# Late products of a fused attention and feed-forward kernel: four PSUM tiles of one bank in place of two tiles of two banks

## The chip, the core and the metric

The kernel runs on one core of a Trainium2 chip. A core has a matrix engine (TensorE, called PE in the profile, with its weight loads as PEld), three engines that work on vectors (VectorE or DVE, ScalarE or ACT, GpSimd or POOL), and SyncE (SP), which here issues the DMAs. PE writes its results into PSUM, a small memory of eight banks; a bank holds 512 float32 values in each of 128 partitions. VectorE and ScalarE read them from there. The metric is the time of one execution on the device in microseconds (us), as the median over executions.

## The reference

Two blocks follow each other. The first is a gated linear recurrence over 768 steps for 4 batches and 8 heads with a head dimension of 48; the second is a feed-forward network with a product of two branches.

```python
f = 1.0 / (1.0 + np.exp(-f_logit))
for t in range(S):
    state = f[:, :, t, :, None] * state + np.einsum('bhd,bhe->bhde', k[:, :, t], v[:, :, t])
    y[:, :, t] = np.einsum('bhd,bhde->bhe', q[:, :, t], state)
...
x = np.ascontiguousarray(y.transpose(0, 2, 1, 3)).reshape(B * S, H * D)   # 3072 x 384
a = x @ w1                    # 3072 x 1024
b = x @ w2
h = a * b @ w3
return (h @ w_out).astype(np.float32)
```

The inputs of attention are float32. The four weights arrive as float64 and are turned into float32 on the core (`fetch`, L1378) before they are used. The result is float32.

## The kernel before, in words

**Stages.** The 3072 tokens are 24 units of 128 tokens (`u`), six for each batch, and six blocks of 512 tokens (`n`). Attention works unit by unit: products of keys and queries inside a unit, a mask, products with the values, and a state that is carried to the next unit. When four units are done, their outputs form a block, and the feed-forward network works on the block. The weights w3 and w_out are multiplied with each other once (`fold`), so that only one output product per block remains.

The feed-forward products of a block are computed in one of three ways. Block 0 uses plain products (`part`). Blocks 1 and 2 use a scheme of seven products in place of eight (`seven`, L972). Blocks 3 to 5 use a scheme that combines sums of slices of x and of w into 18 products, each accumulated in a chain, and adds up their results (`many`, L1120; products at L1148, copies out of PSUM by ScalarE at L1169, additions by VectorE at L1192, the final products of a and b at L1204 and L1211). The output of each block comes from `down` (L1232). It opens three banks, named X, Y and Z, with `start`; the products m1 to m7 go through `three` (L894), so that all of them carry line 897 in the profile. ScalarE copies (`k1`, L1269; `c11`, L1282) and VectorE adds (L1275, L1288, L1299, L1305, L1313) empty those banks.

Beside that work, ScalarE reads through all weights again in the late stretch (`ranges`, L1520, lines 1536 and 1540) to judge whether their size allows this way of computing; if not, a general path is run afterwards.

**The order.** The order of all instructions is written by a planner (`Plan`). A task names its engine, an estimated cost, a priority, what it depends on, and what it takes and frees of counted resources. The planner lists the tasks in time by these estimates, and the loop at L1626 emits them in that order; the program keeps it on every engine. The waits between engines are added afterwards from what each instruction reads and writes of the kernel's tiles.

**The banks.** The resource "f" counts places in PSUM. It has four places (`NF`) during attention, each a tile of one bank in the pool `ps_f`, with the names f0 to f3. The other four banks belong to attention: the pool `ps` has two tiles, `pa` and `py`, each of two banks (`[P, 2, NQ]` with `NQ` = 512). The tile pa holds the products of keys and queries (L579) and the updates of the state (L686), py the outputs of a unit (L653, L672). When the last unit is planned (`u == NU - 1`, L1601 to L1605), four more places are added to "f". They come free when that unit's last tasks on pa and py end: `y` (ScalarE's copy at L845), `mid` (VectorE, L759), `m` (ScalarE, L703) and `v`.

A product that gets one of the first four places asks `ps_f` for a new tile at each opening. A product that gets a later place gets a half of a tile that was made once, at the first such product, and is used by all that follow: places 4 and 5 are the two halves of `pa`, places 6 and 7 the two halves of `py`. The function that hands out the places is `bank` (L378). It runs while instructions are emitted, when the order is already fixed:

```python
if plan.got >= NF:
    nm = ("pa", "py")[(plan.got - NF) // 2]
    if nm not in found:
        found[nm] = ps.tile([P, 2, NQ], F32, name=nm)
    return found[nm][:, plan.got % 2]
return ps_f.tile([P, TB], F32, name=f"f{plan.got}")
```

In the profile the late products into these four banks therefore stand under the names pa and py, with the lines 993 (`seven`), 1148 (`many`) and 897 (`down`); the names do not tell the half. In these rows a product 256 columns wide is written twice side by side and read as 512 wide, and a product of `down` is 192 wide.

Of the kernel before, what the change touches and what calls it, by code (L numbers as in the profile page):

```python
# [36 lines left out]
F32 = mybir.dt.float32  # L37
# [8 lines left out]
P = 128  # L46
# [9 lines left out]
TB = 512  # L56
# [3 lines left out]
NQ = HP * C  # L60
# [3 lines left out]
NF = 4  # L64
# [185 lines left out]
@with_exitstack  # L250
def kernel(
    ctx: ExitStack,
    tc: tile.TileContext,
    q: bass.AP,
    k: bass.AP,
    f_logit: bass.AP,
    v: bass.AP,
    w1: bass.AP,
    w2: bass.AP,
    w3: bass.AP,  # L260
    w_out: bass.AP,
    leaf_mask: bass.AP,
    out: bass.AP,
):
    nc = tc.nc
    const = ctx.enter_context(tc.tile_pool(name="const", bufs=1))
    ident = const.tile([P, P], F32, name="ident")
    w12 = const.tile([P, 2, 2, KM, KH * P], F32, name="w12")
    wc = const.tile([P, KF, DM], F32, name="wc")
    left = const.tile([1, 1], I32, name="left")  # L270
    with tc.manual_schedule():
        outside = ranged(tc, q, k, f_logit, v, w1, w2, w3, w_out, out, ident, w12, wc, left)
        with tc.If(outside > 0, preferred_fallthrough_block=True, label="general"):
            if w1.dtype != F32:
                convert(tc, w1, w2, w3, w_out, w12, wc)
            general(tc, q, k, f_logit, v, leaf_mask, out, ident, w12, wc)
# [17 lines left out]
def ranged(ctx, tc, q, k, f_logit, v, w1, w2, w3, w_out, out, ident, w12, wc, left):  # L294

    nc = tc.nc
    PSUM = bass.MemoryType.PSUM
# [7 lines left out]
    outs = ctx.enter_context(tc.tile_pool(name="outs", bufs=4))  # L305
    one = ctx.enter_context(tc.tile_pool(name="one", bufs=1))
    dram = ctx.enter_context(tc.tile_pool(name="dram", bufs=3, space=bass.MemoryType.DRAM))
    ps = ctx.enter_context(tc.tile_pool(name="ps", bufs=1, space=PSUM))
    ps_f = ctx.enter_context(tc.tile_pool(name="ps_f", bufs=1, space=PSUM))

    floors = keep.tile([P, NQ], F32, name="floor")
    floor = floors[0:R]
# [45 lines left out]
    found = {}  # L358
# [7 lines left out]
    plan = Plan()  # L366
# [11 lines left out]
    def bank():  # L378

        if plan.got >= NF:  # L380
            nm = ("pa", "py")[(plan.got - NF) // 2]
            if nm not in found:
                found[nm] = ps.tile([P, 2, NQ], F32, name=nm)
            return found[nm][:, plan.got % 2]
        return ps_f.tile([P, TB], F32, name=f"f{plan.got}")

    def temporary(i):
# [196 lines left out]
    def turn(u):  # L584

        s = st[u]
        if u < NPE:
            s["py"] = ps.tile([P, 2, NQ], F32, name="py")
            s["pk"] = s["py"][:, :, 2 * C : 2 * C + 2 * R]
        else:  # L590
            s["pk"] = bank()[:, 0 : HP * R].rearrange("p (b r) -> p b r", b=2)
        for hp in range(HP):
            nc.tensor.transpose(  # L593
                out=s["pk"][:, hp // 2, hp % 2 * R : hp % 2 * R + R], in_=s["K"][:, hp * C : hp * C + C],
                identity=ident[0:R, 0:R],
            )

    def first_values(u):

        s = st[u]  # L600
        opens = u % NCH == 0
        s["yb"] = bank().rearrange("p (h c) -> p h c", c=C)[0:R]
        for hp in range(HP):
            for par in range(2):
                h = 2 * hp + par
                w = 64 if par == 0 else D
                nc.tensor.matmul(
                    s["yb"][64 * par : 64 * par + w, hp], lhsT=s["v"][:, h * D : h * D + w],
                    rhs=s["A"][:, par, hp], start=hp == 0, stop=opens, skip_group_check=True,
                )  # L610
        if not opens:
            for hp in range(HP):
                nc.tensor.matmul(
                    s["yb"][:, hp], lhsT=sb[(u - 1) % 2][:, hp], rhs=s["Q"][:, hp * C : hp * C + C],
                    start=False, stop=True, skip_group_check=True,
                )
# [151 lines left out]
    def rest(u):  # L768
# [102 lines left out]
        def moved():  # L871
            s["px"] = bank()[:, 0 : KM * C].rearrange("p (k c) -> p k c", c=C)
            for i, (kc, hp) in enumerate(met):
                nc.tensor.matmul(
                    s["px"][:, kc], lhsT=perm[:, i], rhs=s["ys"][:, hp], start=i % 2 == 0, stop=i % 2 == 1,
                )
# [710 lines left out]
    for u in range(NU):  # L1587
# [13 lines left out]
        if u == NU - 1:  # L1601
            late = plan.add("none", 0.0, lambda: None)
# [408 lines left out]
```

## Time and profile before

| what | value |
| --- | --- |
| median of 4 runs | 463.29 us (463.14 to 463.96) |
| the profiled execution | 463.43 us |
| its span, first to last instruction | 461.7 us, mean granted TensorE clock 0.998 |
| PE busy over the span | 453.4 us |
| VectorE, ScalarE, GpSimd busy | 361.6, 208.8, 66.0 us |
| last unit's copy out of py (L845) | starts at 255.62 us |
| first late product into pa, into py | 264.21 us, 267.66 us |
| last product ends | about 457.3 us |

All times inside the span are counted from its first instruction. A row of the timeline gives a start, a length, the engine, the line, the operation, what is written and what is read (`out<-in`), the shape and how many instructions were merged into the row. In square brackets stands how long the engine was idle before the row and what released it. The list of waits gives, for an engine and a line, who was waited for, the total in us, how often, and the longest wait. The table by stretch gives the window, its length, and for PE, PEld, DVE, ACT and POOL the busy time and the number of instructions, then the granted clock, the share of DMA time and the GB/s moved. Matmuls are pipelined, so one that takes 0.38 us can follow the one before after less than that.

### The profile page before, as it was taken

What the parts mean: (1) busy time and instruction counts of PE and PEld (TensorE: products, weight loads), DVE (VectorE), ACT (ScalarE), POOL (GpSimd) and SP (SyncE); (2) the same over time, 40 slices, a digit from 0 to 9 for tenths busy, and PEclk for the clock granted to TensorE, in tenths of its full rate; (3) what the DMA queues carried; (4) which work ended last, traced back from release to release, by engine and by line L of the source; (5) the groups of instructions that cost most, each with busy time, mean ns of one, the idle gap of its engine ahead of it and who ended that gap; (6) DMA issues with size and microseconds to landing.
All of it is one profiled execution on the core that took longest, in us unless ns stands there. A gap on an engine that the chain in (4) does not pass through costs nothing.

```text
span 461.7 us, 11749 instructions
## 1 busy us (share of the span) xinstructions
PE 453.4 (98%) x4800; PEld 395.9 (86%) x4800; DVE 361.6 (78%) x633; ACT 208.8 (45%) x468; POOL 66.0 (14%) x90
## 2 busy tenths in 40 slices
PE   8999999999999999999999999999999999999996
PEld 6788885666899888889998888998898988889995
DVE  8996999999898999988983599895658566868551
ACT  3565334432234453443323256575665666673000
POOL 9340000121223431223222000000000000000000
PEclk9999999999999999999999999999999999999999
DMA  6997898833246764356323326643265523200111
GB/s 182 280 317 229 310 331 288 267 105 104 70 111 185 209 179 135 102 140 185 99 65 99 128 87 212 214 150 117 97 193 173 179 84 92 92 2 0 36 69 39
DMA packets 43309, 68.75 MB, mean 149 GB/s; under 512 B 5217, under 2 KB 28386, under 8 KB 42226
## 3 DMA queue, kind: packets, MB, share of 16 engines
q1 hardware_dynamic: 43250, 67.95, 47.8%
q8 instruction: 39, 0.64, 0.6%
q14 instruction: 20, 0.16, 0.1%
HBM read 58.88 MB, written 9.04 MB: 147 GB/s over the span
## 4 chain that ended last, share of the span: by engine, by line
PE 95%; DVE 2%; SPq 1%; DMA 1%; issue 0%; POOL 0%; POOLq 0%; DVEq 0%
PE f L897 25%; PE f L993 15%; PE f L1148 11%; PE f L1464 9%; PE py L1148 6%; PE pa L1148 5%; PE py L897 4%; PE pa L897 4%; PE py L653 3%; PE pa L579 2%; PE pa L686 2%; PE f L593 2%; PE py L672 2%; PE py L993 1%; PE f L399 1%; SPq L492 1%
## 5 line engine op out<-in xcount | busy, mean ns | idle before, releaser
L709 POOL TENSOR_SCALAR_AFFINE_SELECT A<-A 64x512 f32<-64x512 f32 (+1 forms) x46 | 43.8, 952 | 109.3 <-ACT A L703 107.1
L1464 PE MATMUL f<-place 128*128 128x384 f32 x128 | 42.4, 487 | 0.0
L897 PE MATMUL f<-xt,w 128*128 128x256 f32 x192 | 42.1, 380 | 0.0
L897 PEld LDWEIGHTS f<-xt,w 128*128 128x128 f32 x192 | 36.3, 190 | 5.0
L1464 PEld LDWEIGHTS f<-place 128*128 128x128 f32 x128 | 23.9, 190 | 15.5
L993 PE MATMUL f<-xt,w 128*128 128x256 f32 x140 | 36.2, 380 | 0.0
L897 PE MATMUL f<-place 128*128 128x192 f32 x192 | 34.8, 327 | 0.0
L897 PEld LDWEIGHTS f<-place 128*128 128x128 f32 x192 | 31.5, 190 | 0.3 <-issue 0.2
L548 DVE TENSOR_TENSOR_SCAN bwd<-gate,back 112x512 f32<-112x512 f32 x24 | 30.4, 1267 | 0.7
L526 DVE TENSOR_TENSOR_SCAN fwd<-gate,floor 112x512 f32<-112x512 f32 x24 | 30.0, 1251 | 1.1 <-ACT gate L518 0.2
L993 PEld LDWEIGHTS f<-xt,w 128*128 128x128 f32 x140 | 26.3, 190 | 3.5
L845 ACT ACTIVATE ys<-py 112x512 f32<-112x512 f32 x22 | 13.1, 596 | 32.6 <-PE py L672 29.7
L1400 ACT ACTIVATE place<-place 128x512 f32<-128x512 uint32 (+2 forms) x24 | 21.4, 890 | 9.8 <-DMA place<-in_w_dram 7.9
L897 PE MATMUL f<-wc,ab 128*128 128x192 f32 x128 | 23.6, 328 | 0.0
L809 POOL TENSOR_TENSOR G<-lasts,gate 112x4 f32<-112x4 f32 x20 | 11.6, 582 | 75.6 <-ACT lasts L531 30.2
L993 PE MATMUL f<-place 128*128 128x256 f32 x84 | 22.4, 385 | 0.0
L518 ACT ACTIVATE gate<-f 112x512 f32<-112x512 f32 x22 | 13.9, 632 | 17.4 <-DMA f<-in_f_logit_dram 8.1
L897 PEld LDWEIGHTS f<-wc,ab 128*128 128x128 f32 x128 | 21.3, 190 | 0.4
L653 PEld LDWEIGHTS py<-A,vt 64*64 64x64 f32 (+1 forms) x672 | 13.3, 127 | 7.3 <-issue 6.5
L653 PE MATMUL py<-A,vt 64*64 64x64 f32 (+1 forms) x672 | 18.1, 223 | 0.2
L1540 ACT ACTIVATE A<-A,back 128x512 f32<-128x512 f32 x23 | 17.9, 780 | 0.2
L1262 DVE TENSOR_TENSOR place<-ab 128x512 f32<-128x512 f32 x24 | 16.6, 690 | 1.0 <-PE f L897 0.9
(355 smaller groups left out, 1046.1 us busy)
## 6 DMA issues: line engine op xcount, KB each, us to landing
place<-in_w_dram SPq DMA_DIRECT2D x21, 512.0 KB, 6.4
A<-in_w_dram SPq DMA_DIRECT2D x19, 512.0 KB, 3.8
place<-in_w_dram SPq DMA_DIRECT2D x8, 1024.0 KB, 6.6
q<-in_q_dram SPq DMA_DIRECT2D x46, 96.0 KB, 2.8
vt<-in_v_dram SPq DMA_DIRECT2D x23, 192.0 KB, 3.4
out_dram<-o SPq DMA_DIRECT2D x23, 192.0 KB, 2.2
k<-in_k_dram SPq DMA_DIRECT2D x44, 96.0 KB, 2.4
yt<-ys SPq DMA_DIRECT2D x44, 96.0 KB, 2.7
```

The costliest lines, as they stand in the source:

```text
L518: nc.scalar.activation(gate[u % 2][:, 0:NQ], fu, AF.Sigmoid)
L526: nc.vector.tensor_tensor_scan(s["P"], gate[u % 2][:, 0:NQ], floor, 0.0, ALU.mult, ALU.max)
L548: nc.vector.tensor_tensor_scan(s["R"][:, ::-1], gate[u % 2][:, NQ:0:-1], back[:, ::-1], 0.0, ALU.mult, ALU.max)
L653: done = nc.tensor.matmul(y_block(u, hp, par, half)[p0 : p0 + w], lhsT=s["v"][half * W : half * W + W, h * D : h * D + w], rhs=s["A"][half ...
L709: nc.gpsimd.affine_select(out=a, in_=a, pattern=pattern, compare_op=ALU.is_ge, fill=0.0, base=0, channel_multiplier=-1,)
L897: nc.tensor.matmul(out_, lhsT=lhs[i], rhs=rhs[i], start=start and i == 0, stop=i == len(lhs) - 1, skip_group_check=True,)
L993: nc.tensor.matmul(q[nm][:, which * TH : which * TH + TH], lhsT=lhs[i](which), rhs=rhs[i], start=start and which == 0 and i == 0, stop=i = ...
L1148: nc.tensor.matmul(banks[g, c][:, which * TH : which * TH + TH], lhsT=lhs, rhs=x_node(a), start=first and which == 0, stop=True, skip_grou ...
L1262: nc.vector.tensor_tensor(abs_[j], x, y, op)
L1400: nc.scalar.activation(part_.bitcast(F32), part_, AF.Copy, bias=2.0, scale=2.0**-51)
L1464: nc.tensor.matmul(w3s["p", jc], lhsT=w3s[jc][:, kc * P : kc * P + P], rhs=wos[:, kc], start=(kc == 0), stop=(kc == KF - 1),)
L1540: return lambda: nc.scalar.activation(a, a, AF.Sign, bias=small, accum_out=counts[:, i : i + 1])
```

## The change

The pools are opened in another order, `ps_f` first, and `ps` is opened in an exit stack of its own, so that it can be closed early. At the first late product, `bank` closes `ps`, and a pool `ps_late` is opened on the banks that come free. From then on each product that gets one of the places 4 to 7 asks `ps_late` for a new tile of one bank, named l4 to l7, as the products in the first four places do with `ps_f`. The planner, its resources and the order of the instructions are not touched.

```diff
-    ps = ctx.enter_context(tc.tile_pool(name="ps", bufs=1, space=PSUM))
     ps_f = ctx.enter_context(tc.tile_pool(name="ps_f", bufs=1, space=PSUM))
+    pairing = ExitStack()
+    ps = pairing.enter_context(tc.tile_pool(name="ps", bufs=1, space=PSUM))
...
     def bank():
 
         if plan.got >= NF:
-            nm = ("pa", "py")[(plan.got - NF) // 2]
-            if nm not in found:
-                found[nm] = ps.tile([P, 2, NQ], F32, name=nm)
-            return found[nm][:, plan.got % 2]
+            if "late" not in found:
+                pairing.close()
+                found["late"] = ctx.enter_context(tc.tile_pool(name="ps_late", bufs=1, space=PSUM))
+            return found["late"].tile([P, TB], F32, name=f"l{plan.got}")
         return ps_f.tile([P, TB], F32, name=f"f{plan.got}")
```

## The prediction

> **What bounds the kernel now.** I read the page first: engine shares, slices, chain.
>
> ```profile
> PE 453.4 (98%) x4800; PEld 395.9 (86%) x4800; DVE 361.6 (78%) x633; ACT 208.8 (45%) x468; POOL 66.0 (14%) x90
> ...
> PE   8999999999999999999999999999999999999996
> ...
> PE 95%; DVE 2%; SPq 1%; DMA 1%; issue 0%; POOL 0%; POOLq 0%; DVEq 0%
> ```
>
> TensorE is busy 98% of the span and 95% of the chain that ended last is its work. Only an interval in which PE stands still can be won. So the second view is the list of waits of PE in the late stretch, 262 us to the end, which is all that the change touches:
>
> ```profile
> PE py L897 <- DVE ys L1192: 0.6, 1, 0.6
> ```
>
> It has one entry: one product into py, waiting once, for a VectorE addition. The busy table by stretch says the same:
>
> ```profile
> 256.30:457.26 200.96, 200.39 (x1038) 184.00 (x1036) 138.06 (x282) 103.64 (x241) 0.00 (x0) 1.00 0.34 110
> ```
>
> The first number after the window is its length, the second PE's busy time: 0.57 us idle in 201 us, at a full clock (1.00). The third view is the timeline around that place:
>
> ```profile
> 352.89 1.89 PE L1148 MATMUL f<-place,f 128*128 128x256 f32 x8
> ...
> 353.16 0.69 DVE L1192 TENSOR_TENSOR a<-pa,a 128x512 f32<-128x512 f32 x1 [0.98 <-PE pa L1148]
> ...
> 354.61 0.69 DVE L1192 TENSOR_TENSOR ys<-ys,py 128x512 f32<-128x512 f32 x1
> ...
> 355.35 1.57 PE L897 MATMUL py<-wc,ab 128*128 128x192 f32 x8 [0.57 <-DVE ys L1192]
> ```
>
> The x8 group before the hole spans 1.89 us and one matmul lasts 0.379 (the row of L1148), so its starts are (1.89 - 0.379) / 7 = 0.216 us apart. Its last start is 352.89 + 7 x 0.216 = 354.40, and the next product could have begun at 354.62. It began at 355.35, when the addition that reads py ended (354.61 + 0.69 = 355.30).
>
> Is that wait a need of the data? The product at 355.35 is the first of an output block (m1 in `down`). It opens a bank, so it only needs that bank's last reader. The rows of py just before tell which one that was:
>
> ```profile
> 336.88 1.03 PE L1148 MATMUL py<-xt,q 128*128 128x256 f32 x4
> ...
> 346.83 1.46 PE L897 MATMUL py<-place,ab 128*128 128x192 f32 x8
> 348.63 0.35 DVE L1305 TENSOR_TENSOR o<-py,place 128x192 f32<-128x192 f32 x1
> ```
>
> Two products live in py at once: the 512-wide one, last written at 336.88 and read only at 354.61, and a 192-wide output product that opened, grew and was read (348.63 to 348.98) in between. One bank cannot hold both, so they are py's two halves. The half with the output product was free from 348.98 on; its operand ab was complete before too, since the sums over the same ab (L1262) had run by 348.71 (348.02 + 0.69). The wait at 355.35 is for the other half. The tie between the halves shows a second time, 40 us earlier:
>
> ```profile
> 311.84 1.03 PE L1148 MATMUL py<-place,floor 128*128 128x256 f32 x4
> ...
> 312.91 0.36 DVE L1313 TENSOR_TENSOR o<-py,place 128x192 f32<-128x192 f32 x1 [1.81 <-PE py L1148]
> 313.30 0.59 ACT L1169 COPY ys<-py 128x512 f32<-128x512 f32 x1 [3.15 <-DVE o L1313]
> ```
>
> VectorE, with the output product complete, stands until a product in the other half ends; then ScalarE, which only reads, waits for VectorE, which only reads. A tile of two banks is guarded as one thing where the halves' uses overlap.
>
> **The change, part by part.**
>
> *The tie goes.* Each late product now has a tile of its bank alone. At 355.35 PE no longer waits for the addition: 355.35 - 354.62 = 0.73 us. The group behind the hole also took 1.57 us where the same group takes 1.46 elsewhere (346.83), because its weights were loaded only as the wait ended: 0.11 us more. Sum 0.84.
>
> *Near misses.* Where ScalarE is held behind VectorE as above, its copy lands just before PE's next accumulation into that bank: the copy from pa at 386.27 ends 386.86 and the product starts at 387.00, and of the eight matmuls pa<-xt,fwd the longest takes 391 ns against a median of 379. Some four such places at 10 to 15 ns: 0.05 us. I take it in.
>
> *What is late next.* VectorE has no idle row from 353.16 to its addition L1288 at 362.15, which PE's product at 362.82 waits for; VectorE stood 0.60 us before 362.15, so it is free at 361.55. With PE 0.84 earlier, the product would be due at 361.98 and L1288 would end at 361.55 + 0.36 = 361.91: still in time, with 0.07 in hand. And VectorE itself gets the 0.98 us back that it stood at 353.16 for a product in pa while it read the half that was not being written. I take a loss of 0, with 0.3 as the upper end should VectorE run late all the same. Further on the waits for ScalarE's copies are 0.9 us short of mattering in the regular pattern (a copy of 0.59 us starts as PE begins the following product, and PE comes back two products of 0.86 later).
>
> *Freed waits of VectorE and ScalarE.* In this stretch they are busy 138.06 and 103.64 of 200.96 us. PE waits for them nowhere else, so what they gain is worth nothing on the path. Covered by PE's work.
>
> *New tile per product.* 33 products open in pa and py after 262 us. Each of them becomes a fresh tile that must wait for the release of the one before in its bank, by all that touched it, PE itself included. Lower end: nothing, as for the products in f, which already work so; their groups run at the same 0.216 and (1.46 - 0.326) / 7 = 0.162 us as those in pa and py, with 0.0 idle. Upper end: every opening loses its overlapped weight load as at 355.35, 33 x 0.11 = 3.6 us. Below nothing it cannot go, since a wait added gives no time back. I take nothing; f is the same operation on the same engine.
>
> *The hand-over.* The pool of pa and py closes and the new one opens on its banks, so the first late product may wait for all of attention's readers: the last is ScalarE's copy L845, 255.62 to 256.31. The first product into pa starts at 264.21. Cover 7.9 us, cost nothing; without the planner's own hold on these four slots it would be at most that.
>
> *Order and queues.* `bank()` is called when the order is already fixed, so no instruction changes its place on PE, DVE, ACT, POOL or SP; no DMA is added or moved. The order of the two PSUM pools changes, so the tiles sit in other banks; all eight are in use before and after. Bounds 0 and 0.
>
> Sum: 0.84 + 0.05 = 0.89 us. The profiled execution took 463.43 us: 461.7 of span and 1.73 around it, which stays. 463.43 - 0.89 = 462.54. The median of the runs shown is 463.29, 0.14 below it: 462.4.
>
> A rule against reading it so. PE's starts 0.216 and 0.162 us apart in f, pa and py alike say that it works at its own rate and only the hole is to be had, 0.89 us. The Trainium skill ("Perfetto Trace Analysis", section "Identifying the Most-Contended Engine") calls matmul busy time a poor measure of headroom and asks for the share of weight loads instead. By it the late stretch has 200.96 - 184.00 = 16.96 us of room, and a change that loosens waits could win up to that.
>
> **The rivals.**
>
> *No change.* The halves are not what ties them, or the released tile carries the same wait: 463.3. For it: the profile names tiles, not banks. Against it: rows 311.84 to 313.30, where one reader waits for another.
>
> *Slower: openings pay.* Each of the 33 openings loses the prefetched weight load, 3.6 us: 463.29 - 0.89 + 3.6 = 466.0. It decides against the change from 0.89 / 0.11 = 8 openings on. For it: after the hole the load was late by 0.11. Against it: the openings in f.
>
> *Larger gain.* Freed engines let PE close more than I see. PE has 0.57 us idle by the table and 0.89 by its starts; more would need stops that neither shows. The tail behind 457.26 (last addition 457.30, last store issued 457.69) is a chain behind PE and only shifts. If as much again as the 0.89 went: 461.5.
>
> **How the numbers follow.** 0.2% of 463.29 is 0.93 us, about what a measurement of this kernel can tell from no change, and the forecast of 0.89 lies on that line. Chances: forecast 0.74 (462.1 to 462.8, the 0.3 of VectorE and the spread of the runs), larger gain 0.06, no change 0.10, openings pay 0.10. Of the forecast's 0.74 I put 0.42 beyond 0.93 us, since a freed VectorE and ScalarE can only remove further small misses, and 0.32 short of it. Faster 0.42 + 0.06 = 0.48, same 0.32 + 0.10 = 0.42, slower 0.10. The range takes in no change and leaves out the larger gain and most of the slower case: 462.0 to 463.6.
>
> **What would show it.** In the profile after: the list of PE's waits after 262 us without the row for py L897, the output group near 354.6 at 1.46 us instead of 1.57, and all later rows 0.8 to 0.9 us earlier; no row in which ACT L1169 is released by a DVE addition that only reads another product; idle before the late products 0.0. Wrong would be: a new row of PE waiting at an opening, gaps at 264, or the group at 362 starting late behind L1288.

## The result and the profile after

The changed kernel takes 462.46 us (median of 33 runs), the kernel before 463.35 us (median of 53). The ratio is 0.998, with a 95% interval of 0.9973 to 0.9987: a gain of 0.9 us, clear of zero, and just short of the 0.2% (0.93 us) that the prediction took as the line between faster and no change. Forecast was 462.4 us.

The profiled execution after the change took 462.61 us with a span of 460.8 us. Its page, in the lines that answer to those of before (engines, PE's slices, the chain by engine):

```profile
PE 452.6 (98%) x4800; PEld 396.3 (86%) x4800; DVE 362.4 (79%) x633; ACT 208.6 (45%) x468; POOL 67.8 (15%) x90
...
PE   7999999999999999999999999999999999999996
...
PE 95%; POOL 2%; DVE 1%; issue 0%; POOLq 0%; DVEq 0%
```

Nothing of the picture changes at this scale: the same 4800 matmuls, PE busy 98%. The difference stands in PE's waits. Before, the late stretch had one. This is the whole list of PE's waits after the change, over the whole span (engine, line, who was waited for; then us in total, times, longest):

```profile
PE f L400 <- DVE floor L423: 1.7, 1, 1.7
PE py L594 <- DVE K L557: 0.6, 1, 0.6
PE pa L687 <- issue: 0.6, 1, 0.6
PE f L594 <- DVE K L557: 0.4, 1, 0.4
```

All four belong to attention and its start; the lines are one higher than before, since the diff adds a line above them. The late stretch has none left. Its row in the table by stretch (window, length, PE busy, PEld, DVE, ACT, POOL, clock, DMA share, GB/s):

```profile
256.30:456.40 200.10, 200.10 (x1038) 184.66 (x1037) 138.24 (x282) 104.07 (x242) 0.00 (x0) 1.00 0.34 111
```

PE was idle 0.57 us of 200.96 before, and is idle 0.00 of 200.10 now. The two windows do not hold quite the same work, because attention took 0.12 us longer in this execution: the first late product starts at 264.33, where it was 264.21. Counted from the start of the first late product to the end of the last product (457.27 before, 456.51 now), PE's same 1000 matmuls take 193.06 us before and 192.18 now, 0.88 us less. This stretch is free of attention's small differences, and the experiments below are compared by it too.

The timeline around the hole:

```profile
352.14 1.03 PE L1149 MATMUL l<-place,bwd 128*128 128x256 f32 x4
352.22 0.68 DVE L1193 TENSOR_TENSOR a<-l,a 128x512 f32<-128x512 f32 x1
...
353.01 1.89 PE L1149 MATMUL f<-place,f 128*128 128x256 f32 x8
...
353.66 0.69 DVE L1193 TENSOR_TENSOR ys<-ys,l 128x512 f32<-128x512 f32 x1
...
354.73 1.46 PE L898 MATMUL l<-wc,ab 128*128 128x192 f32 x8
```

Two things moved. The output group starts 354.73 - 353.01 = 1.72 us after the group before it, where it was 355.35 - 352.89 = 2.46: 0.74 us. And it takes 1.46 us in place of 1.57: 0.11 us. That is 0.85 of the 0.88 us. The other 0.03 are three matmuls, at 387.00, 400.83 and 404.29 before, that took 391, 387 and 392 ns; no matmul of their groups takes more than 380 now. The second movement around the hole is easy to pass over: VectorE's first addition, a<-l,a, now starts at 352.22, beside the product with bwd that PE is just writing to the other bank. Before, it started at 353.16, after 0.98 us of standing, 0.27 us after the matching PE group ahead of the hole. It now starts 0.79 us ahead of that group (353.01). So the addition that PE used to wait for ends at 354.35, before PE arrives.

The other place that the prediction showed has lost its two ties:

```profile
311.96 1.03 PE L1149 MATMUL l<-place,floor 128*128 128x256 f32 x4
312.16 0.36 DVE L1314 TENSOR_TENSOR o<-l,place 128x192 f32<-128x192 f32 x1 [0.94 <-PE l L898]
...
313.03 0.58 ACT L1170 COPY ys<-l 128x512 f32<-128x512 f32 x1 [2.73 <-PE l L1149]
```

VectorE is released by the output product that it reads (L898), and starts at 312.16, while PE writes the other bank; before it waited until that write had ended. ScalarE is released by the product that it reads, and no longer by VectorE.

### The profile page after: what moved, and what is told of

It is laid out like the page before. It is cut to its first block, busy times and chain, and to the rows that moved or that the text cites. A ratio compares the mean times of both kernels' runs of the same rounds, so it can differ in the third digit from the quotient of the medians.

```text
span 460.8 us, 11785 instructions
## 1 busy us (share of the span) xinstructions
PE 452.6 (98%) x4800; PEld 396.3 (86%) x4800; DVE 362.4 (79%) x633; ACT 208.6 (45%) x468; POOL 67.8 (15%) x90
## 4 chain that ended last, share of the span: by engine, by line
PE 95%; POOL 2%; DVE 1%; issue 0%; POOLq 0%; DVEq 0%
PE f L898 25%; PE f L994 15%; PE f L1149 11%; PE l L1149 11%; PE f L1465 9%; PE l L898 8%; PE py L654 3%; PE pa L580 2%; PE pa L687 2%; PE f L594 2%; PE l L994 2%; PE py L673 2%; POOL ab L438 1%; PE f L400 1%; DVE K L557 0%
## 5 line engine op out<-in xcount | busy, mean ns | idle before, releaser
L898 PE MATMUL f<-xt,w 128*128 128x256 f32 x192 | 42.1, 380 | 0.0
L898 PEld LDWEIGHTS f<-xt,w 128*128 128x128 f32 x192 | 36.4, 190 | 4.9
L898 PE MATMUL f<-place 128*128 128x192 f32 x192 | 34.8, 327 | 0.0
L898 PEld LDWEIGHTS f<-place 128*128 128x128 f32 x192 | 31.5, 190 | 0.3 <-issue 0.2
L810 POOL TENSOR_TENSOR G<-lasts,gate 112x4 f32<-112x4 f32 x20 | 12.6, 630 | 76.3 <-ACT lasts L532 28.9
L898 PE MATMUL f<-wc,ab 128*128 128x192 f32 x128 | 23.6, 328 | 0.0
L898 PEld LDWEIGHTS f<-wc,ab 128*128 128x128 f32 x128 | 21.3, 190 | 0.4
L654 PE MATMUL py<-A,vt 64*64 64x64 f32 (+1 forms) x672 | 18.1, 223 | 0.2
```

The costliest lines, as they stand in the source:

```text
L654: done = nc.tensor.matmul(y_block(u, hp, par, half)[p0 : p0 + w], lhsT=s["v"][half * W : half * W + W, h * D : h * D + w], rhs=s["A"][half ...
L898: nc.tensor.matmul(out_, lhsT=lhs[i], rhs=rhs[i], start=start and i == 0, stop=i == len(lhs) - 1, skip_group_check=True,)
```

## The experiments

All edits are to the changed kernel, in `bank` unless said otherwise. Ratios are to the kernel before, measured on the same chip in the same series.

**Which tie makes the hole.** The prediction laid the wait to the two halves of py (theory A). The timeline after the change offers a rival (theory B): that VectorE came late at all was the doing of the tie between the halves of pa, and the tie of py only handed this on. Each pair can be put back alone.

`py_split` ties pa's halves again:

```diff
-            return found["late"].tile([P, TB], F32, name=f"l{plan.got}")
+            if plan.got < NF + 2:
+                if "lpa" not in found:
+                    found["lpa"] = found["late"].tile([P, 2, NQ], F32, name="lpa")
+                return found["lpa"][:, plan.got % 2]
+            return found["late"].tile([P, TB], F32, name=f"l{plan.got}")
```

> The changed kernel, with the halves of pa in one tile of two banks again and only the two banks of py split. Theory A (the hole at 355 us is made by the tie between the halves of py alone) and theory B (two ties in series make it: that of pa holds VectorE for 0.98 us, that of py hands the delay on to PE) both expect the whole gain: 0.84 to 0.89 us below the kernel before, ratio 0.998, and no wait of PE after 262 us. If the gain comes from something else that the four tiles bring, it is less than half.

Measured: 462.44 us against 463.71, ratio 0.9977 (0.9959 to 0.9995); no wait of PE after 256 us. The whole gain, as both theories have it. VectorE is still held for 0.98 us, and its addition starts as late as before, but PE, which writes another bank, no longer waits for it:

```profile
353.15 0.69 DVE L1197 TENSOR_TENSOR a<-lpa,a 128x512 f32<-128x512 f32 x1 [0.98 <-PE lpa L1153]
...
354.60 0.69 DVE L1197 TENSOR_TENSOR ys<-ys,l 128x512 f32<-128x512 f32 x1
354.61 1.46 PE L902 MATMUL l<-wc,ab 128*128 128x192 f32 x8
```

`pa_split` is the same edit with `plan.got >= NF + 2` and a tile `lpy`, so that py's halves are tied and pa's are not.

> The changed kernel, with the halves of py in one tile again and only the two banks of pa split. Theory A expects the time of the kernel before, ratio 1.000, with PE waiting 0.6 us or more at 354.7 for the addition that reads py. Theory B expects the whole gain, ratio 0.998: PE still has the wait for that addition, but VectorE is no longer held at 353.16, runs the addition 0.95 us earlier, and ends it some 0.4 us before PE arrives.

Measured: 462.98 us against 463.71, ratio 0.998 (0.9964 to 0.9996). The interval excludes 1.000, which theory A expected. The timeline of this kernel shows how:

```profile
352.94 1.03 PE L1153 MATMUL l<-place,bwd 128*128 128x256 f32 x4
353.02 0.68 DVE L1197 TENSOR_TENSOR a<-l,a 128x512 f32<-128x512 f32 x1
...
353.81 1.89 PE L1153 MATMUL f<-place,f 128*128 128x256 f32 x8
...
354.46 0.69 DVE L1197 TENSOR_TENSOR ys<-ys,lpy 128x512 f32<-128x512 f32 x1
...
355.53 0.33 PE L902 MATMUL lpy<-wc,ab 128*128 128x192 f32 x1
```

VectorE runs beside the product with bwd, its addition out of lpy ends at 355.15, and PE comes for the other half of lpy at 355.53, 1.72 us after the start of the group before, as in the changed kernel. The tie of py is still there and costs nothing.

**The waits by themselves.** If theory B holds, putting back PE's wait alone must cost nothing, and putting back both waits must bring the hole back, in a kernel whose tiles are all split.

`one_wait` (in `down`, `m1`; the reader is the last addition emitted that reads place 7):

```diff
+WAITS_AT = (3, 1)
...
             def m1():
+                if (n, i) == WAITS_AT:
+                    ordered(nc.tensor.nop(), found["reader"])
                 three(start("X"), each(quarter_(0, 0)), b(0, 0))
```

> The changed kernel, with one wait put back: PE, before the output product near 354.7 us, waits for the addition that reads the other bank (the one that it waited for before the change). Theory A expects the time of the kernel before, ratio 1.000. Theory B expects nothing, ratio 0.998, since in the changed kernel that addition ends at 354.35 and PE arrives at 354.73.

`two_waits` adds, behind the addition in `many` (which is now kept as `done_`), a wait for the last matmul of the product with bwd, kept in `found`:

```diff
+                    if (n, g, i, j) == (4, 0, 10, 11):
+                        ordered(done_, found["mm", 4, 0, 9])
```

> As with one wait, and a second wait put back: VectorE's addition a<-l,a, which reads one bank of the old pa, waits for the product with bwd in the other bank, which ended at 353.05 before the change. Theories A and B both expect the hole to be back: PE waits 0.6 us near 354.7, ratio 1.000 (0.999 to 1.001). If it stays at 0.998, neither tie is what the change took away.

Measured: one wait 462.46 us, ratio 0.9975 (0.996 to 0.9991); two waits 463.72 us, ratio 0.9999 (0.9981 to 1.0018). With one wait the addition ends at 353.87 + 0.69 = 354.56, before PE arrives, and PE stands nowhere:

```profile
353.87 0.69 DVE L1194 TENSOR_TENSOR ys<-ys,l 128x512 f32<-128x512 f32 x1
...
354.95 0.81 PE L899 MATMUL l<-wc,ab 128*128 128x192 f32 x4
```

With both waits the rows of before return, the 0.98 us of VectorE included:

```profile
353.38 1.89 PE L1150 MATMUL f<-place,f 128*128 128x256 f32 x8
353.65 0.69 DVE L1194 TENSOR_TENSOR a<-l,a 128x512 f32<-128x512 f32 x1 [0.98 <-PE l L1150]
...
355.11 0.69 DVE L1194 TENSOR_TENSOR ys<-ys,l 128x512 f32<-128x512 f32 x1
...
355.94 0.89 PE L899 MATMUL l<-wc,ab 128*128 128x192 f32 x4 [0.66 <-DVE ys L1194]
```

Theory A falls, theory B stands: two ties in series, and either one taken away is worth the whole hole. The medians of these series differ by some tenths of a us for other reasons. The stretch from the first late product to the last says the same more sharply, in one profiled execution of each kernel:

| kernel | same 1000 matmuls, us |
| --- | --- |
| before | 193.06 |
| `pool_alone` (below: both pairs tied) | 193.06 |
| `two_waits` | 193.08 |
| `pa_split` (py tied) | 192.20 |
| `py_split` (pa tied) | 192.20 |
| `one_wait` | 192.18 |
| after | 192.18 |

The 0.02 that `pa_split` and `py_split` have over the changed kernel are the long matmuls named above: with py tied the one at 404.29 is back (392 ns), with pa tied the other two (392 and 387 ns).

**The rest of the change.** `pool_alone` keeps the new order of the pools, the early closing and the new late pool, and puts two tiles of two banks into it:

```diff
-            return found["late"].tile([P, TB], F32, name=f"l{plan.got}")
+            nm = ("lpa", "lpy")[(plan.got - NF) // 2]
+            if nm not in found:
+                found[nm] = found["late"].tile([P, 2, NQ], F32, name=nm)
+            return found[nm][:, plan.got % 2]
```

> The changed kernel's new order of pools, its early closing of the old pool and its new late pool, but in the new pool two tiles of two banks again. If the split of the halves is the whole cause: the time of the kernel before, ratio 1.000 (0.999 to 1.001), with PE waiting 0.6 us near 354.7. If the other banks or the hand-over from pool to pool have a share, the ratio moves towards 0.998.

Measured: 463.39 us against 463.54, ratio 1.0001 (0.9992 to 1.001), and the old row in PE's list of waits:

```profile
PE lpy L901 <- DVE ys L1196: 0.6, 1, 0.6
```

The other banks and the hand-over from pool to pool have no share.

`kept_tiles` makes four tiles of one bank once and uses them for all late products:

```diff
-            return found["late"].tile([P, TB], F32, name=f"l{plan.got}")
+            nm = f"l{plan.got}"
+            if nm not in found:
+                found[nm] = found["late"].tile([P, TB], F32, name=nm)
+            return found[nm]
```

> The changed kernel with four tiles of one bank that are made once and used by all late products, in place of a new tile at each of the 33 openings. If an opening with a new tile costs nothing, as the prediction took it: the time of the changed kernel, ratio 0.998, and no wait of PE after 262 us. If openings cost something (up to 0.11 us each), this is faster than the changed kernel, by 3.6 us at most: ratio 0.990 to 0.998.

`after_again` is the changed kernel itself, as a measure in the same series.

> The changed kernel, on the same chip as the other three, as their measure: ratio 0.998 to the kernel before.

Measured: kept tiles 462.61 us, ratio 0.9981 (0.9972 to 0.999); the changed kernel 462.63 us, ratio 0.9983 (0.9974 to 0.9992). The 1000 matmuls take 192.18 us in both. A new tile at each opening costs nothing that can be seen. What counts is one bank to a tile, not a tile to a product.

**More ties.** `four_tied` goes the other way and puts the four late banks into one tile:

```diff
-            return found["late"].tile([P, TB], F32, name=f"l{plan.got}")
+            if "l" not in found:
+                found["l"] = found["late"].tile([P, 4, NQ], F32, name="l")
+            return found["l"][:, plan.got - NF]
```

> The changed kernel with all four late banks in one tile, so that every use of one bank is ordered against every use of the other three. If ties cost only where a reader is late: ScalarE's copies out of the four banks wait for each other's products; some ten of them would end 0.08 us before PE comes for the next product, each of which costs about 0.08 as at 285 us, and the delayed copies pass delays on to VectorE: 1 to 6 us over the changed kernel, ratio 1.000 to 1.011 to the kernel before. If ties cost nothing in general and the hole was a single accident, the ratio stays at 0.998 to 1.000.

Measured: 480.66 us, ratio 1.037 (1.0355 to 1.0384): 17 us over the kernel before and 18 over the changed one, three times the upper end that I had given. The longest entries of PE's list of waits after 256 us, and the stretch up to PE's last product:

```profile
PE l L1151 <- ACT ys L1172: 2.3, 4, 1.2
PE l L1151 <- ACT a L1172: 1.8, 2, 1.5
PE l L996 <- ACT A L1543: 1.5, 1, 1.5
PE l L1151 <- ACT Q L1172: 1.3, 3, 0.7
PE l L900 <- DVE place L1291: 0.9, 2, 0.5
```

```profile
256.30:475.10 218.80, 207.25 (x1040) 182.72 (x1040) 138.33 (x282) 102.86 (x242) 0.00 (x0) 1.00 0.32 101
```

PE is idle 218.80 - 207.25 = 11.55 us. The same 1000 matmuls as above take 210.32 us, 18.1 more than in the changed kernel; 11.55 of them are this idle time, and PE's busy time is 198.77 - 192.18 = 6.6 us higher. At the hole of the kernel before, both parts of such a loss can be seen: PE stood 0.73 us by its starts, of which 0.57 count as idle (the other 0.16 are the tail of the last matmul, which the next one otherwise overlaps), and the group behind took 0.11 longer. At 0.16 + 0.11 a stop, the 18 stops of the whole list would give 4.9 us (an estimate); where the rest goes stays open.

Two things I had priced too low. The first is ScalarE's copies. PE waits ten times for one of them (the three entries of L1172, and a fourth of L1037 with 0.5 us). That is as many as I had expected, but they come to 5.9 us in all, 0.6 each and not 0.08. In the longest of these waits the readers stand in a row, VectorE for PE's product, ScalarE for VectorE, PE for ScalarE:

```profile
409.73 1.03 PE L1151 MATMUL l<-xt,k 128*128 128x256 f32 x4
410.87 0.69 DVE L1195 TENSOR_TENSOR Q<-ys,l 128x512 f32<-128x512 f32 x1 [1.32 <-PE l L1151]
...
411.59 0.59 ACT L1172 COPY a<-l 128x512 f32<-128x512 f32 x1 [2.13 <-DVE Q L1195]
...
412.23 1.13 PE L1151 MATMUL l<-xt,w 128*128 128x256 f32 x4 [1.47 <-ACT a L1172]
```

The second, smaller part I had not priced at all. It is in the timeline where the output block is emptied:

```profile
316.03 0.36 DVE L1302 TENSOR_TENSOR o<-l,place 128x192 f32<-128x192 f32 x1 [0.99 <-PE l L900]
...
316.44 1.57 PE L900 MATMUL l<-wc,place 128*128 128x192 f32 x8 [0.45 <-DVE o L1302]
...
318.05 0.36 DVE L1308 TENSOR_TENSOR o<-l,place 128x192 f32<-128x192 f32 x1 [0.87 <-PE l L900]
...
318.46 1.13 PE L1151 MATMUL l<-place,floor 128*128 128x256 f32 x4 [0.45 <-DVE o L1308]
```

With one tile, PE and the reader take turns: VectorE may not read one bank until PE's product in another has ended, and PE may not write the next product until VectorE has read. In these rows each turn costs PE 0.45 us of standing for a reading of 0.36, and late weights, also where no reader would be late. The four waits of this kind (L1291, L1302 and L1308) come to 1.8 us. The other four stops of the list, 3.9 us, stay unexplained here. I had priced only the places where a reader ends just before PE comes.

## Why the prediction was right, and where its reasoning was not

- *The forecast.* 463.35 - 462.46 = 0.89 us between the medians; the sum was 0.89 us, and the trace gives 0.74 + 0.11 + 0.03 = 0.88. The range held. That the medians agree to 0.01 is luck: the interval of the ratio allows 0.6 to 1.25 us. I had put the larger share (0.42 of 0.74) beyond 0.93 us, for further small misses that freed engines would remove; the gain lies below that line, and the trace shows no such miss beyond the 0.03.
- *"The wait at 355.35 is for the other half."* Right as to the wait, and its price: 0.74 us for the start and 0.11 for the group, against 0.73 and 0.11.
- *"The tie goes" laid to py's halves.* Right that this tie is enough to explain the gain, for splitting py alone gives all of it (0.9977); incomplete as a cause. The row that carries the other half was in my own fence, the addition at 353.16 with 0.98 us of standing for PE's product in pa, and I counted it only as time that VectorE gets back further on. Splitting pa alone, with py still tied, gives the whole gain (0.998), and PE's wait alone, put back, costs nothing (0.9975). The hole needs both ties, and I had named one. The gain was right because cutting either is enough, and the change cuts both.
- *Near misses, 0.05 us.* Borne out, a little smaller: three such places and not four, at 12, 8 and 12 ns over the usual 379 or 380, 0.03 us. After the change no matmul of these groups takes more than 380 ns, and with one pair tied again only that pair's places return. Run times alone could not tell 0.03 us.
- *"What is late next."* I took no loss, with 0.07 us in hand at the addition L1288. Measured: that addition (L1289 now) starts at 361.43 and ends at 361.79, and PE's product starts at 362.10, so 0.31 us are in hand. VectorE even stands 0.83 us before it, for PE's product. The case that my 0.07 was reckoned for, PE early and VectorE still held at pa, is `py_split`: there the addition starts without a pause at 361.46, ends at 361.81, and PE's product starts at 361.97. So 0.16 us are in hand and the loss is 0, as I took it.
- *Openings and hand-over at nothing.* Right: ratios 0.9981 and 0.9983 with and without new tiles, and 1.0001 for the pools alone. The trace after has 11785 instructions in place of 11749. The difference is all in semaphore instructions (37 more on ScalarE, 6 fewer on VectorE, 5 more with PE's weight loads), and PE's stretch shows no trace of it.
- *The rivals.* No change and the price at openings are refuted by these runs. Of a larger gain there is nothing: PE has no late wait left to lose, and but for one start that comes 0.08 us late at 285.05, as it did before, its starts from 262 us on lie 0.216 or 0.162 us apart throughout. The 16.96 us of room by weight loads were a wrong reading: they count time in which loads overlap only once. The loads' own lengths, added up, are 196.6 us in the 200.96 of the stretch before, which leaves 4.3. Of that, too, only 0.88 was won here; whether another change could use the rest no run tells.

## What to carry to other kernels

Where two banks of PSUM hold unrelated products, give each a tile of its own: a reader of one half and a writer of the other are otherwise ordered, and so are two readers. What that costs in this kernel is set less by the number of ties than by whether they hang together into a chain that reaches the busiest engine. Against one bank to a tile, two banks cost 0.2% here (463.54 to 462.63 us in one series), four cost 3.9% (480.66 us). When a profile shows one wait, ask of the engine waited for why it was late, one row further back, before naming the cause.

## What was not expected of the hardware

PE's stops cost more than their idle time: in the kernel with all four banks tied, 11.55 us of idle time went with 6.6 us more of busy time for the same matmuls at an undiminished clock (1.00). A group of eight matmuls of 192 columns takes 1.46 us when it follows without a stop, and 1.57 us behind one.
